# Float64 tiles five ahead on another queue, block 0's stores moved, and smaller rings in a two-MLP kernel

## The chip, the cores and the metric

The kernel runs on one core of a Trainium2 chip. The metric is the device time of one execution in microseconds (us). The engines are named as in the profile: PE is TensorE's matmul, PEld its weight load, DVE is VectorE, ACT ScalarE, POOL GpSimd, SP SyncE; a q behind the name (ACTq, SPq) is that engine's instruction queue, which also issues DMAs, in its order.

## What is computed

Packed attention in float32 and two gated MLPs over its 4608 rows. The arrays of q, k, v and p are float32; the four weight matrices are float64 (512 x 2048 and back).

```python
def sm_attn(qq, kk, vv):
    s = scale * np.matmul(qq, kk.transpose(0, 1, 3, 2))
    s = s - np.max(s, axis=-1, keepdims=True)
    a = np.exp(s)
    a = a / (np.sum(a, axis=-1, keepdims=True) + 1e-09)
    return np.matmul(a, vv)
p_packed = sm_attn(p, k, v)            # 8 batches x 8 heads, 32 packed rows
out = sm_attn(q, p_packed, p_packed)   # 576 rows, 64 columns a head
x = out.transpose(0, 2, 1, 3).reshape(4608, 512)
h = x @ w_in;  x = (h / (1 + exp(-h))) @ w_out              # first MLP
h = x @ w_in2; y = (h * clip(h + 3, 0, 6) / 6) @ w_out2     # second MLP
```

## The kernel before

**Tiling.** The 4608 tokens are nine blocks of 512. In each block the first MLP runs over NF = 16 slices of 128 hidden columns: three hidden matmuls per product (L820 to L822, into hps), ScalarE's activation (L828) and gate (gh L835, gl DVE L836), three projecting matmuls (L843 to L845, into acc). Each float32 factor is split into a high and a low part, and a product is three matmuls: high by low, low by high, high by high. Attention for the coming batches is woven between these groups by a planner (it interleaves by place and cost; the order on TensorE is the same before and after the change).

**Block 0 converts the first MLP's weights.** Feed goes through 32 keys, alternately ("in", f) and ("out", f). load_raw (L142, DMA at L145) brings a tile of float64 as pairs of int32; conv_begin (L170, L171, ACT), conv_bits (L176, L177, DVE), conv_add (L182, POOL) rebuild a float32; conv_end (L195 ACT the high part, L196 DVE or POOL the low) gives win, wr or wo. One advance works on four neighbouring keys in these states. Feed.ahead says how many keys the loads stand ahead: RAW - 1 = 3, with RAW = 4 tiles of the tag raw. spare_raw takes tiles of the same tag for two small arrays. The split weights that later blocks want are stored to DRAM (w1i and w1o) by keep (L189), one advance or more after their split; next_in (L216, wi) and next_out (L228, wo) load them back. The calls 12 to 15 of block 0 each load one wi tile ahead; next_out waits until all kept stores are issued and the last projections have begun.

**Blocks 1 to 8** load wi and wo as they go. Blocks up to 7 use w_in fused with the packed attention values (fuse_steps, L615 and L616: fused, xf, xh, xl). Beside them Prep converts the second MLP's weights in 32 units: load (L257, praw, two DMAs on ACT), conv_begin, conv_bits, sums for a scheme of seven products, a cast and a difference (hi7 tiles), and three stores w2in or w2out (L301 to L303, on ACT). One step of Prep, some ten to a unit, follows each hidden slice; what is left at the end of block 8 is done at once by prep.end.

**Second** is the second MLP, from 942 us to the end: six pairs of N = 384 tokens each, two times two blocks by seven products. Each pair has a hidden half (28 chunks of 12 matmuls: L1058 to L1060, on xc; then the bank is added on DVE: hu L1020, h L1029, hv L1023, and gated: ACT hr L1004, DVE g L1007), a few operands made ready (t1 L1077, split L1099 ACT and L1100 DVE: ro), and a project half (28 chunks: L1136 to L1138, on ro; outputs o, ou, ov). ws, a ring of WS = 7 chunks of weights, is loaded by SP (L942) one chunk for each used. x_steps makes the next pair's xc: it loads xr (L961), makes three differences (xe, L966 to L970) and splits seven operands (L974, L975), one step at each second chunk of the project half. soon(n, ...) runs a function n steps later.

**Queues.** A DMA is issued by the engine that the code names, in that engine's order. The program gives DMAs the semaphores of eight lanes in turn, over all queues, and a DMA instruction waits for the one that had its lane before. SP also issues q, k, v and p of the coming batches (L317, L327, L334, L338, L345) and the x1d and output stores.

Of the kernel before, what the change touches and what calls it, by code (L numbers as in the profile page):

```python
# [18 lines left out]
def tile_pack_attention_two_mlps(ctx: ExitStack, tc, q, k, v, p, w_in1, w_out1, w_in2, w_out2, out):  # L19
# [77 lines left out]
    def spare_raw():  # L97
        return wp.tile([P, 2 * T], I32, tag="raw", name="raw", bufs=RAW).bitcast(F32)
# [44 lines left out]
    def load_raw(key, src):  # L143
        raw = wp.tile([P, 2 * T], I32, tag="raw", name="raw", bufs=RAW)
        nc.sync.dma_start(out=raw.rearrange("p (a f) -> p a f", a=src.shape[1]), in_=src)  # L145
        raws[key] = raw
# [38 lines left out]
    def keep(behind=1):  # L185

        while len(kept) > behind:
            to, w = kept.pop(0)
            nc.scalar.dma_start(out=to, in_=w)  # L189

    def conv_end(key):
# [4 lines left out]
        (nc.vector if kind == "in" else nc.gpsimd).tensor_sub(out=w[:, 1], in0=v, in1=f32(w[:, 0]))  # L196
        made[key] = w
        if kind == "in":
            kept.append((piece_in(f), f32(w).rearrange("p n (c f) -> p n c f", c=KC)))
        elif f % 2:  # L200
            kept.append((w1o[f].rearrange("n p f -> p n f"), f32(w)))
# [8 lines left out]
    def next_in():  # L210
        if want_in:
            key = want_in.pop(0)
            t = wts.tile([P, 2, DM], F32R, tag="wi", name="wi", bufs=4)
# [7 lines left out]
    projected = [-1]  # L221

    def next_out():

        while want_out and not kept and projected[0] >= NF - 2 and (want_out[0][0] * NF + want_out[0][1]) // 2 <= (projected[0] + 1) // 2 - 1 + WO:
# [11 lines left out]
    class Prep:  # L237
# [671 lines left out]
    WS = 7  # L909

    class Second:
# [41 lines left out]
        def x_steps(self, n):  # L953
# [11 lines left out]
            e = [self.right.tile([P, 2, N], F32, tag=f"xe{i}", name=f"xe{i}") for i in range(3)]  # L965
            nc.vector.tensor_sub(out=e[0], in0=b[1, 1], in1=b[0, 1])  # L966
            nc.vector.tensor_sub(out=b[0, 1], in0=b[0, 1], in1=b[0, 0])
            yield
            nc.vector.tensor_sub(out=e[1], in0=b[1, 1], in1=b[0, 1])
            nc.vector.tensor_sub(out=e[2], in0=b[1, 0], in1=e[1])  # L970
            yield
            for k, v in (1, b[0, 0]), (6, e[1]), (5, b[0, 1]), (7, e[0]), (2, b[1, 0]), (4, e[2]), (3, b[1, 1]):
# [4 lines left out]
                yield  # L977
# [10 lines left out]
        def hidden(self, n):  # L988
# [25 lines left out]
            def after(f, k):  # L1014
# [79 lines left out]

# [337 lines left out]
```

## Time and profile before

| | us |
|---|---|
| runs | 1687.24, 1687.88, 1687.83; median 1687.83 |
| profiled execution | 1691.33 |
| its span | 1689.5 |
| PE busy in the span | 1570.1 (93%) |
| ACT busy | 804.9 (48%) |
| DVE busy | 1039.1 (62%) |
| mean granted clock | 0.977 |

The stages of the profiled execution are: start-up attention to 44 us, block 0 to 196, blocks 1 to 8 to 942, Second to 1689. A row of windows gives an engine's busy time and number of instructions in a stretch, then the granted TensorE clock, in parts of the full one (0.50 and 1.00 are its two levels; a mean in between mixes them), the mean busy share of the 16 DMA engines and what they moved. A row of waits says for which instruction's or transfer's end an engine stood, in sum, how often, and the longest. A row of the timeline ends in the idle time before the instruction and what ended it. Releasers are inferred, and a wait for several is put down to the last.

### The profile page before, as it was taken

Reading aid. Unit: us, or ns where it says so; the run is one execution under the profiler, and the core shown is the slowest. Engines: PE = TensorE matmul, PEld = TensorE weight load, DVE = VectorE, ACT = ScalarE, POOL = GpSimd, SP = SyncE. Lnnn points to the kernel's source line nnn. Section 1 sums busy time; section 2 is a strip of 40 time slices with the busy share of each in tenths; the row PEclk is TensorE's granted clock in tenths of the full one; section 3 lists DMA queues with packets and bytes.
Section 4 is the critical chain, followed back from the end, with each engine's and each line's share of the span. In section 5 each row is a group of like instructions: output and inputs, shape, how many; then the busy total and the mean of one; then the engine's idle time right before and its main releaser. Section 6 shows DMA issues by size and latency. Waiting matters only on the chain.

```text
span 1689.5 us, 23588 instructions
## 1 busy us (share of the span) xinstructions
PE 1570.1 (93%) x8396; PEld 1343.7 (80%) x8396; DVE 1039.1 (62%) x1750; ACT 804.9 (48%) x1356; POOL 216.8 (13%) x188
## 2 busy tenths in 40 slices
PE   5877899889999899999989999999999999999997
PEld 3655656667676677767868999999999999999997
DVE  5645455465556555554343479569578678677675
ACT  4756345555555455555444345345345344444443
POOL 2443311111111021112213000000000000000000
PEclk9999899899999899999999999999999999999999
DMA  7786676776769665766698687787787887887875
GB/s 192 239 254 192 217 213 184 220 209 187 194 181 242 190 195 139 208 218 204 191 311 250 195 274 243 253 294 249 252 294 249 260 286 249 274 271 251 257 252 154
DMA packets 409749, 388.01 MB, mean 230 GB/s; under 512 B 156192, under 2 KB 282144, under 8 KB 409632
## 3 DMA queue, kind: packets, MB, share of 16 engines
q1 hardware_dynamic: 271264, 252.25, 49.6%
q10 hardware_dynamic: 138368, 134.24, 25.6%
q8 instruction: 68, 1.11, 0.3%
q14 instruction: 49, 0.40, 0.1%
HBM read 324.53 MB, written 61.87 MB: 229 GB/s over the span
## 4 chain that ended last, share of the span: by engine, by line
PE 55%; DVE 16%; ACT 13%; DMA 8%; issue 3%; POOL 2%; ACTq 1%; SPq 1%; DVEq 0%; POOLq 0%
PE acc L843 5%; PE b L1137 5%; PE acc L844 5%; PE b L1138 5%; PE acc L845 5%; PE b L1136 5%; PE b L1058 4%; PE b L1060 4%; PE b L1059 4%; PE hps L820 3%; ACT hr L1004 3%; DVE g L1007 3%; PE hps L822 3%; PE hps L821 3%; DVE ro L1100 2%
## 5 line engine op out<-in xcount | busy, mean ns | idle before, releaser
L1058 PE MATMUL b<-xc,ws 128*128 128x384 f32 x672 | 229.4, 341 | 8.0 <-DVE hu L1020 8.0
L1137 PE MATMUL b<-ro,ws 128*128 128x384 f32 x672 | 227.1, 338 | 6.2 <-DVE ro L1100 6.2
L1138 PE MATMUL b<-ro,ws 128*128 128x384 f32 x672 | 225.9, 336 | 0.0
L1136 PE MATMUL b<-ro,ws 128*128 128x384 f32 x672 | 225.8, 336 | 0.0
L1060 PE MATMUL b<-xc,ws 128*128 128x384 f32 x672 | 225.1, 335 | 0.0
L1059 PE MATMUL b<-xc,ws 128*128 128x384 f32 x672 | 224.8, 335 | 0.0
L836 DVE TENSOR_TENSOR gl<-hps,gh 128x512 fp32r<-128x512 f32 x144 | 99.1, 688 | 201.0 <-ACT gh L835 201.0
L1099 ACT CAST ro<-g 128x768 fp32r<-128x768 f32 x168 | 137.3, 835 | 116.9 <-DVE g L1089 34.9
L1100 DVE TENSOR_TENSOR ro<-g,ro 128x768 fp32r<-128x768 f32 x168 | 158.0, 953 | 23.7 <-ACT ro L1099 21.0
L1058 PEld LDWEIGHTS b<-xc,ws 128*128 128x128 f32 x672 | 126.2, 188 | 13.5 <-DVE hu L1020 13.4
L1137 PEld LDWEIGHTS b<-ro,ws 128*128 128x128 f32 x672 | 126.3, 188 | 9.7 <-DVE ro L1100 9.7
L828 ACT ACTIVATE hps<-hps 128x512 f32<-128x512 f32 x144 | 84.1, 584 | 95.6 <-PE hps L822 70.2
L1059 PEld LDWEIGHTS b<-xc,ws 128*128 128x128 f32 x672 | 126.3, 188 | 0.0
L1138 PEld LDWEIGHTS b<-ro,ws 128*128 128x128 f32 x672 | 126.3, 188 | 0.0
L1136 PEld LDWEIGHTS b<-ro,ws 128*128 128x128 f32 x672 | 126.3, 188 | 0.0
L1060 PEld LDWEIGHTS b<-xc,ws 128*128 128x128 f32 x672 | 126.1, 188 | 0.0
L843 PE MATMUL acc<-gh,wr 128*128 128x512 f32 x288 | 120.5, 418 | 0.9 <-ACT gh L835 0.9
L843 PE MATMUL acc<-gh,wo 128*128 128x512 f32 x288 | 117.9, 409 | 2.9 <-ACT gh L835 2.9
L844 PE MATMUL acc<-gl,wr 128*128 128x512 f32 x288 | 115.3, 400 | 0.3 <-DVE gl L836 0.2
L844 PE MATMUL acc<-gl,wo 128*128 128x512 f32 x288 | 114.2, 397 | 0.9 <-DVE gl L836 0.8
L845 PE MATMUL acc<-gh,wr 128*128 128x512 f32 x288 | 114.6, 398 | 0.0
L845 PE MATMUL acc<-gh,wo 128*128 128x512 f32 x288 | 113.8, 395 | 0.0
(262 smaller groups left out, 3046.3 us busy)
## 6 DMA issues: line engine op xcount, KB each, us to landing
ws<-w2in SPq DMA_DIRECT2D x336, 256.0 KB, 3.9
ws<-w2out SPq DMA_DIRECT2D x336, 256.0 KB, 3.5
wi<-w1i ACTq DMA_DIRECT2D x80, 512.0 KB, 4.8
wo<-w1o ACTq DMA_DIRECT2D x64, 512.0 KB, 4.7
x1d<-x SPq DMA_DIRECT2D x18, 512.0 KB, 3.2
raw<-in_moe_w_in_dram SPq DMA_DIRECT2D x16, 512.0 KB, 5.2
raw<-in_moe_w_out_dram SPq DMA_DIRECT2D x16, 512.0 KB, 4.7
w1i<-win ACTq DMA_DIRECT2D x16, 512.0 KB, 5.3
```

Source lines behind the costliest of these rows:

```text
L836: nc.vector.tensor_sub(out=gl, in0=g, in1=f32(gh))
L843: mm(acc[e], lhsT=w[:, 0, s], rhs=gh, start=first, stop=False)
L844: mm(acc[e], lhsT=w[:, 0, s], rhs=gl, start=False, stop=False)
L845: mm(acc[e], lhsT=w[:, 1, s], rhs=gh, start=False, stop=last)
L1058: mm(ps, lhsT=wh, rhs=xs[k][:, 0, c], start=first, stop=False, skip_group_check=True)
L1059: mm(ps, lhsT=wh, rhs=xs[k][:, 1, c], start=False, stop=False, skip_group_check=True)
L1060: mm(ps, lhsT=wl, rhs=xs[k][:, 0, c], start=False, stop=last, skip_group_check=True)
L1099: nc.scalar.copy(out=t[:, 0], in_=v)
L1100: nc.vector.tensor_sub(out=t[:, 1], in0=v, in1=f32(t[:, 0]))
L1136: mm(acc[i], lhsT=wh, rhs=ro[:, 0, f], start=first, stop=False, skip_group_check=True)
L1137: mm(acc[i], lhsT=wh, rhs=ro[:, 1, f], start=False, stop=False, skip_group_check=True)
L1138: mm(acc[i], lhsT=wl, rhs=ro[:, 0, f], start=False, stop=last, skip_group_check=True)
```

## The change

Tiles of ("out", f) keys and the two spare arrays go to a tag of their own, raw2, with three buffers, so that raw and raw2 have seven together; loads stand five keys ahead, up to two in one advance, and after the start-up ScalarE's queue issues them. Stores of kept split weights move from ScalarE's queue to SyncE's. wi has five buffers; five next_in calls stand at 20 to 24. next_out goes by the state of the call before. Prep starts five steps later, hi7 has two buffers. In Second, ws has six buffers; x_steps has one buffer xe, differences made in place, and 11 steps instead of 9; t1 runs at 2 steps instead of 3, and split is two parts, at 3 and 5 instead of 4; the steps of x_steps fall on other chunks of the project half.

```diff
     def spare_raw():
-        return wp.tile([P, 2 * T], I32, tag="raw", name="raw", bufs=RAW).bitcast(F32)
+        return win0.tile([P, 2 * T], I32, tag="raw2", name="raw2").bitcast(F32)
...
     def load_raw(key, src):
-        raw = wp.tile([P, 2 * T], I32, tag="raw", name="raw", bufs=RAW)
-        nc.sync.dma_start(out=raw.rearrange("p (a f) -> p a f", a=src.shape[1]), in_=src)
+        if key[0] == "in":
+            raw = wp.tile([P, 2 * T], I32, tag="raw", name="raw", bufs=RAW)
+        else:
+            raw = win0.tile([P, 2 * T], I32, tag="raw2", name="raw2")
+        (nc.sync if early[0] else nc.scalar).dma_start(out=raw.rearrange("p (a f) -> p a f", a=src.shape[1]), in_=src)
...
             to, w = kept.pop(0)
-            nc.scalar.dma_start(out=to, in_=w)
+            nc.sync.dma_start(out=to, in_=w)
...
-            t = wts.tile([P, 2, DM], F32R, tag="wi", name="wi", bufs=4)
+            t = wts.tile([P, 2, DM], F32R, tag="wi", name="wi", bufs=5)
...
-    projected = [-1]
+    projected = [-1, -1]
...
-        while want_out and not kept and projected[0] >= NF - 2 and (want_out[0][0] * NF + want_out[0][1]) // 2 <= (projected[0] + 1) // 2 - 1 + WO:
+        now, projected[1] = projected[1], -1 if kept else projected[0]
+        while want_out and now >= NF - 2 and (want_out[0][0] * NF + want_out[0][1]) // 2 <= (now + 1) // 2 - 1 + WO:
...
             self.load(0)
-            yield
+            for _ in range(6):
+                yield
...
-                hi = self.pool.tile([P, S7, P], F32, tag="hi7", name="hi7")
+                hi = self.pool.tile([P, S7, P], F32, tag="hi7", name="hi7", bufs=2)
...
-    WS = 7
+    WS = 6
...
                     if f % 2:
-                        soon(3, lambda: self.t1(f // 2))
-                        soon(4, lambda: self.split(f // 2))
+                        soon(2, lambda: self.t1(f // 2))
+                        soon(3, lambda: self.split_hi(f // 2))
+                        soon(5, lambda: self.split_lo(f // 2))
...
-                if self.prep and s % 2 == 0 and s >= 4:
+                if self.prep and s and s // FD % 2 == 0:
                     next(self.prep, None)
...
-            if self.loaded < i + self.ahead:
-                self.load()
+            for _ in range(2):
+                if self.loaded < i + self.ahead:
+                    self.load()
...
-    feed.ahead = RAW - 1
+    feed.ahead = RAW + 1
...
-                    if 12 <= calls[0] < 16:
+                    if 20 <= calls[0] < 25:
                         next_in()
```

split_hi and split_lo are the two halves of split, ACT's cast and DVE's difference. In x_steps the three differences and seven splits are:

```diff
-            e = [self.right.tile([P, 2, N], F32, tag=f"xe{i}", name=f"xe{i}") for i in range(3)]
-            nc.vector.tensor_sub(out=e[0], in0=b[1, 1], in1=b[0, 1])
-            nc.vector.tensor_sub(out=b[0, 1], in0=b[0, 1], in1=b[0, 0])
-            yield
-            nc.vector.tensor_sub(out=e[1], in0=b[1, 1], in1=b[0, 1])
-            nc.vector.tensor_sub(out=e[2], in0=b[1, 0], in1=e[1])
-            yield
-            for k, v in (1, b[0, 0]), (6, e[1]), (5, b[0, 1]), (7, e[0]), (2, b[1, 0]), (4, e[2]), (3, b[1, 1]):
...
+            nc.vector.tensor_sub(out=e, in0=b[1, 1], in1=b[0, 1])
+            yield
+            nc.vector.tensor_sub(out=b[0, 1], in0=b[0, 1], in1=b[0, 0])
+            yield
+            split(1, b[0, 0])
+            yield
+            nc.vector.tensor_sub(out=b[0, 0], in0=b[1, 1], in1=b[0, 1])
+            yield
+            split(6, b[0, 0])
...
```

**ACT in block 0**, in the middle of the conversions, before (cr is the tile under conversion, hps and gh the activation and gate of a hidden slice, wr and win split weights, ppT a copy for attention):

```order
L828 ACTIVATE hps<-hps 128x512
L835 CAST gh<-hps 128x512
L189 DMA w1o_115<-wo 128x2x512
L195 CAST wr_1015<-cr 128x512
L216 DMA wi<-w1i_109 128x1024
L170 ACTIVATE cr<-raw 128x512
L171 ACTIVATE cr<-raw 128x512
L104 COPY ppT<-abank 128x256
```

and with the change, where line numbers lie three to seven further on:

```order
L835 ACTIVATE hps<-hps 128x512
L842 CAST gh<-hps 128x512
L148 DMA raw_1016<-in_moe_w_out_dram 128x1024
L198 CAST wr_1019<-cr 128x512
L173 ACTIVATE cr<-raw 128x512
L174 ACTIVATE cr<-raw 128x512
L104 COPY ppT<-abank 128x256
L148 DMA raw<-in_moe_w_in_dram 128x4x256
L198 CAST win<-cr 128x512
```

The store of w1o and the load of wi are gone, and loads of float64 tiles stand before the casts of split weights. **SP in the same stretch**, before, with buffer numbers (vt, nat and qt hold the coming batches' v, k and q):

```order
L317 DMA vt_983<-in_v_dram 64x4x64
L327 DMA nat_985<-in_v_dram 128x2x256
L327 DMA nat_987<-in_v_dram 128x2x256
L317 DMA qt_989<-in_q_dram 64x4x64
L338 DMA nat_991<-in_q_dram 128x4x64 x2
L338 DMA nat_994<-in_q_dram 128x4x64 x2
L145 DMA raw_1012<-in_moe_w_in_dram 128x4x256
L145 DMA raw_1044<-in_moe_w_out_dram 128x1024
L145 DMA raw_1076<-in_moe_w_in_dram 128x4x256
L145 DMA raw_1121<-in_moe_w_out_dram 128x1024
L334 DMA nat_1141<-in_k_dram 32x16x32 x4
```

and with the change:

```order
L324 DMA vt_987<-in_v_dram 64x4x64
L334 DMA nat_989<-in_v_dram 128x2x256
L334 DMA nat_991<-in_v_dram 128x2x256
L324 DMA qt_993<-in_q_dram 64x4x64
L345 DMA nat_995<-in_q_dram 128x4x64 x2
L345 DMA nat_998<-in_q_dram 128x4x64 x2
L192 DMA w1o5_115<-wo_920 128x2x512
L192 DMA w1i1_110<-win_949 256x4x128
L192 DMA w1i2_111<-win_1048 256x4x128
```

Stores of split weights (w1o and w1i) stand among the loads of q, k and v, where the loads of float64 tiles (raw) stood. **DVE in the hidden half of a pair of Second**, before (g is a gated half of an operand, ro a split operand, hu, hv and h sums of the hidden products):

```order
L1007 SCALAR_TENSOR_TENSOR g_9576<-hr,hu 128x384
L1023 TENSOR_TENSOR hv<-h_9727,b 128x384
L1024 TENSOR_TENSOR hv<-hv,b 128x384
L1007 SCALAR_TENSOR_TENSOR g_9582<-hr,hv 128x384
L1077 TENSOR_TENSOR g_9576<-g_9576,g_9575 128x768
L1100 TENSOR_TENSOR ro<-g_9575,ro 128x768
L1007 SCALAR_TENSOR_TENSOR g_9579<-hr,b 128x384
L1020 TENSOR_TENSOR hu<-h_9810,b 128x384
L1029 TENSOR_TENSOR h_9727<-h_9727,b 128x384
```

and with the change (L1103 is t1, L1032 the gate, L1128 the low half of split, L1045 hu):

```order
L1032 SCALAR_TENSOR_TENSOR g_9569<-hr,hu 128x384
L1048 TENSOR_TENSOR hv<-h_9720,b 128x384
L1049 TENSOR_TENSOR hv<-hv,b 128x384
L1103 TENSOR_TENSOR g_9569<-g_9569,g_9568 128x768
L1032 SCALAR_TENSOR_TENSOR g_9575<-hr,hv 128x384
L1032 SCALAR_TENSOR_TENSOR g_9572<-hr,b 128x384
L1045 TENSOR_TENSOR hu<-h_9804,b 128x384
L1128 TENSOR_TENSOR ro<-g_9568,ro 128x768
L1054 TENSOR_TENSOR h_9720<-h_9720,b 128x384
```

t1 stands one gate earlier, and the low half of ro behind the next subtraction into hu instead of before the gate.

## Rows read from the trace of the kernel before

**Rows 1.** Windows by stage; columns: us, busy by engine (count), granted clock, DMA share, GB/s

```profile
44.00:196.00 152.00, 121.67 (x573) 89.00 (x573) 89.34 (x128) 91.75 (x166) 66.70 (x49) 0.92 0.73 222
...
210.00:942.00 732.00, 688.05 (x3421) 517.05 (x3420) 382.06 (x763) 368.33 (x634) 126.83 (x118) 0.98 0.72 205
942.00:1690.00 748.00, 724.62 (x4181) 714.27 (x4179) 541.41 (x800) 323.31 (x517) 14.18 (x6) 1.00 0.79 256
```

**Rows 2.** Waits of PE, 44 to 210 us: waited for, total us, times, longest

```profile
PE abank L487 <- ACT ppT L104: 4.7, 1, 4.7
PE abank L365 <- DVE gl L836: 4.6, 1, 4.6
...
PE abank L496 <- DVE xf L616: 3.3, 1, 3.3
...
PE abank L609 <- ACT ppT L104: 2.6, 1, 2.6
...
PE hps L820 <- ACT d L101: 2.4, 1, 2.4
```

**Rows 3.** Waits of ACT before L170, 44 to 200 us

```profile
ACT cr L170 <- DMA raw<-in_moe_w_out_dram: 7.6, 2, 5.2
ACT cr L170 <- DMA wi<-w1i: 7.5, 1, 7.5
...
ACT cr L170 <- DMA raw<-in_moe_w_in_dram: 6.5, 1, 6.5
```

**Rows 4.** Windows of three stretches behind waits of PE

```profile
106.70:113.40 6.70, 5.41 (x14) 2.87 (x14) 4.35 (x7) 6.34 (x12) 1.95 (x2) 0.50 0.93 310
...
175.00:181.60 6.60, 6.24 (x18) 4.88 (x19) 4.96 (x7) 4.40 (x9) 4.36 (x3) 0.50 0.81 263
205.70:212.30 6.60, 6.38 (x16) 4.37 (x16) 0.45 (x2) 2.11 (x4) 0.61 (x1) 0.50 0.75 265
```

**Rows 5.** Timeline of ACT, blocks 0 to 1: start, us, instruction, [idle before <-releaser]

```profile
204.46 0.58 ACT L835 CAST gh<-hps 128x512 fp32r<-128x512 f32 x1 [4.85 <-DMA w1o<-wo]
...
210.19 0.67 ACT L170 ACTIVATE pr<-praw 128x512 f32<-128x512 f32 x1 [5.14 <-DMA praw<-in_moe_w_in_dram]
```

**Rows 6.** Waits of PE in the two-MLP part

```profile
PE b L1058 <- DVE hu L1020: 8.0, 12, 1.0
PE b L1137 <- DVE ro L1100: 6.2, 11, 0.8
```

**Rows 7.** Timeline of DVE at one wait of the hidden half

```profile
980.37 0.56 DVE L1007 SCALAR_TENSOR_TENSOR g<-hr,hv 128x384 f32<-128x384 f32 x1 [0.74 <-ACT hr L1004]
980.85 0.95 DVE L1077 TENSOR_TENSOR g<-g,g 128x768 f32<-128x768 f32 x1
981.95 0.96 DVE L1100 TENSOR_TENSOR ro<-g,ro 128x768 fp32r<-128x768 f32 x1
...
983.28 0.55 DVE L1020 TENSOR_TENSOR hu<-h,b 128x384 f32<-128x384 f32 x1
```

**Rows 8.** Timeline of PE and its weight load in the project half

```profile
1026.61 0.19 PEld L1137 LDWEIGHTS b<-ro,ws 128*128 128x128 f32 x1 [0.63 <-DVE ro L1100]
1026.61 0.44 PE L1137 MATMUL b<-ro,ws 128*128 128x384 f32 x1 [0.32 <-DVE ro L1100]
```

**Rows 9.** Timelines of ACT and PE at two windows of Prep

```profile
553.32 0.66 ACT L170 ACTIVATE pr<-praw 128x512 f32<-128x512 f32 x1 [2.51 <-issue]
...
557.82 0.80 PE L820 MATMUL hps<-a2h,fused 128*128 128x512 f32 x1 [6.08 <-DVE gl L836]
...
595.39 0.59 ACT L101 COPY T<-abank 128x512 f32<-128x512 f32 x1 [0.38 <-PE abank L431]
...
597.46 0.65 PE L451 MATMUL abank<-nat,T 128*32 128x64 f32 x32
```

**Rows 10.** DMA issues, 1340 to 1360 us: count, size, median us to landing

```profile
ws<-w2in SPq DMA_DIRECT2D x14, 256.0 KB, 5.3
```

**Rows 11.** A wait of SP's queue, 44 to 200 us

```profile
SPq L317 <- PE abank L454: 18.8, 2, 9.7
```

More of the change, by code (lines that the diff above doesn't have):

```diff
@@ L195, in conv_end @@
         nc.scalar.copy(out=w[:, 0], in_=v)
-        (nc.vector if kind == "in" else nc.gpsimd).tensor_sub(out=w[:, 1], in0=v, in1=f32(w[:, 0]))
         made[key] = w
         if kind == "in":
+            nc.vector.tensor_sub(out=w[:, 1], in0=v, in1=f32(w[:, 0]))
             kept.append((piece_in(f), f32(w).rearrange("p n (c f) -> p n c f", c=KC)))
-        elif f % 2:
-            kept.append((w1o[f].rearrange("n p f -> p n f"), f32(w)))
+        else:
+            nc.gpsimd.tensor_sub(out=w[:, 1], in0=v, in1=f32(w[:, 0]))
+            if f % 2:
+                kept.append((w1o[f].rearrange("n p f -> p n f"), f32(w)))
     def piece_in(f):
@@ L964, in x_steps, with split @@
             b = {(i, k): xr[:, 2 * i:2 * i + 2, k * N:(k + 1) * N] for i in range(2) for k in range(2)}
-            e = [self.right.tile([P, 2, N], F32, tag=f"xe{i}", name=f"xe{i}") for i in range(3)]
-            nc.vector.tensor_sub(out=e[0], in0=b[1, 1], in1=b[0, 1])
-            nc.vector.tensor_sub(out=b[0, 1], in0=b[0, 1], in1=b[0, 0])
-            yield
-            nc.vector.tensor_sub(out=e[1], in0=b[1, 1], in1=b[0, 1])
-            nc.vector.tensor_sub(out=e[2], in0=b[1, 0], in1=e[1])
-            yield
-            for k, v in (1, b[0, 0]), (6, e[1]), (5, b[0, 1]), (7, e[0]), (2, b[1, 0]), (4, e[2]), (3, b[1, 1]):
+            e = self.right.tile([P, 2, N], F32, tag="xe", name="xe")
+            def split(k, v):
                 t = self.right.tile([P, 2, 2, N], F32R, tag=f"xc{k}", name=f"xc{k}")
@@ L976, in x_steps @@
                 self.x[k] = t
-                yield
+            nc.vector.tensor_sub(out=e, in0=b[1, 1], in1=b[0, 1])
[7 more added lines that the diff above has]
+            split(6, b[0, 0])
+            yield
+            split(5, b[0, 1])
+            yield
+            split(7, e)
+            yield
+            split(3, b[1, 1])
+            yield
+            nc.vector.tensor_sub(out=b[1, 1], in0=b[1, 0], in1=b[0, 0])
+            yield
+            split(2, b[1, 0])
+            yield
+            split(4, b[1, 1])
+            yield
         def begin_step(self):
@@ L1093, in sums, with split_hi, split_lo @@
                 nc.vector.tensor_sub(out=t, in0=b21, in1=t)
+        def split_hi(self, s):
+            t = self.left.tile([P, 2, 2, N], F32R, tag="ro", name="ro", bufs=4)
+            nc.scalar.copy(out=t[:, 0], in_=self.operand(s))
+            self.ro[s] = t
+        def split_lo(self, s):
+            t = self.ro[s]
+            nc.vector.tensor_sub(out=t[:, 1], in0=self.operand(s), in1=f32(t[:, 0]))
         def split(self, s):
             if s < FD * S7:
-                t = self.left.tile([P, 2, 2, N], F32R, tag="ro", name="ro", bufs=4)
-                v = self.operand(s)
-                nc.scalar.copy(out=t[:, 0], in_=v)
-                nc.vector.tensor_sub(out=t[:, 1], in0=v, in1=f32(t[:, 0]))
-                self.ro[s] = t
+                self.split_hi(s)
+                self.split_lo(s)
         def project(self, n):
```

## The prediction

> **What bounds the kernel now.** I read the stages first, then the waits of the busiest engine, then what its releasers waited for. The windows by stage [rows 1] show two kernels in one: in the two-MLP part after 942 us TensorE (PE) is busy 724.6 of 748 us, in blocks 1 to 8 (210 to 942) 688 of 732 us, and in block 0 (44 to 196) only 121.7 of 152 us, 30.3 us idle, with a granted clock of 0.92. So block 0 has the most to give, and the last part has so much TensorE work that only its own small waits count.
>
> In block 0, TensorE's waits [rows 2] name ScalarE (ACT) in three of the rows; in the L496 row DVE's xf is itself fed by ACT. What held ACT is in its own waits [rows 3]: three rows, 21.6 us, all before L170, the first conversion of a float64 tile, all for transfers. (The row that names wi<-w1i I read as a tile's load too: one landed at the same moment.) TensorE's 4.7 us (L487) is the end of the 7.5 us wait, its 2.4 us (L820) lies in the 6.5 us wait, its 2.6 us (L609) in the 5.2 us wait, its 3.3 us (L496) in the 2.4 us wait that makes up the rest of the 7.6. After a wait the engine also runs slower: in the two stretches behind the 4.7 and the 3.3 us the granted clock is 0.50 [rows 4], the lower of its two levels (1.2 of 2.4 GHz), so a stretch of 6.7 us does the work of 3.3.
>
> **Block 0: loads five ahead, on ACT's queue; stores on SP's.** The loads are issued three keys ahead by SyncE (SP), whose queue also carries q, k and v and stops for them: a v load there waited up to 9.7 us for a matmul [rows 11]. In the change they stand in ACT's order two keys earlier, ahead of the converting instructions, and the 24 stores go to SP. What can be removed on TensorE is the sum of the four waits, 4.7 + 2.4 + 2.6 + 3.3 = 13.0 us, and the half-speed stretches behind two of them, 3.35 + 3.3 = 6.7, together 19.7, and some 1.7 for a shorter half-speed stretch behind the 2.4 us wait (an estimate, half of one like those in rows 4): 21. What is added: a load on ACT can itself stand, since a DMA instruction waits for its buffer and for the semaphore it shares with a DMA issued eight earlier in the program. That this can stop ACT is seen at the end of block 0, where the cast of gh, behind two loads of wo in ACT's order, stands 4.85 us for the store of w1o [rows 5]. No row shows it for a load of a float64 tile. The bounds: nothing, or as much as the 21.6 us that go, less what lies beside TensorE work; I take 3 us, near the lower end, because the buffer that a load takes was read two keys earlier at least, and because eight DMAs earlier is two or three keys in most places, longer than most landings (it is less where SP has just issued eight small q or k loads in a row, which the change's order has twice in this stretch). So -18 us, between -5 and -30 (the upper end: some waits of ACT for POOL in the same chain go too, as its instructions come earlier).
> Moving the stores to SP costs nothing on TensorE: they wait there for the split that DVE or POOL makes, and behind them stand loads of q, k and v with the same lead as before. The price if that cover is gone is a late k or v, bounded by 9.7 us [rows 11]; it is in the range.
> The four early wi loads of block 0, moved from its calls 12 to 15 to 20 to 24 and now five, leave the crowded stretch at 107 to 113, where the DMA share is 0.93 [rows 4], and need no other price: they are wanted only in block 1.
>
> **The boundary of blocks 0 and 1.** Today ACT issues the last stores and at once the wo loads, and stands 4.85 us for the last store [rows 5]; TensorE waits 4.6 us at L365 [rows 2] and then runs 6.6 us at clock 0.50 [rows 4], 3.3 lost. Straight after, ACT waits 5.1 us for praw, the first raw tile of Prep [rows 5], which the change loads six steps ahead of its use instead of one. The change keeps the stores off ACT and holds the wo loads back by one call. Gain 4.6 + 3.3 = 7.9, taken as -8; between -3 (the wo tiles, now later, are waited for themselves) and -10.
>
> **Blocks 1 to 8.** Five more yields move all of Prep's work five steps later; the second hi7 buffer and the fifth wi buffer only loosen. The phase matters where Prep's three w2in stores and the two conversions of the next unit fall between the softmax exponentials and the next hps on ACT. Once before, they did: ACT issued for 2.5 us, converted from 553.32 on, and TensorE stood 6.1 us before L820 [rows 9]. In the order of the change the same group stands ahead of the COPY of T in four windows, one of them behind 592. There T is ready at 595.98 and wanted at 597.46 [rows 9], 1.5 us later, and the group (2.5 us of issue and two conversions of 0.66) takes ACT 3 to 4 us; I estimate new stalls of about 5 us in all, and 3 us less at 557.8, where the group is gone. With half-speed stretches the balance is 0, between -8 and +10. The five steps more that are left to the end of block 8 are half a unit, about 3 us of work on ACT, beside TensorE work; in the range.
>
> **The two-MLP part.** In each pair's hidden half TensorE waits before L1058 on DVE: 8.0 us in 12 waits, two in each of the six pairs [rows 6]. The DVE rows before one [rows 7] show why. DVE works in order: the gate at 980.37 stood 0.74 us for ACT, then came t1 (0.95 us), then ro's low half, which could start only at 981.95 when ACT's cast was nearly done, and only then the subtraction that frees the bank, ending at 983.83. The change puts t1 into the wait for ACT, and the low half two steps behind the high one. That takes about a microsecond off each place, so the waits should go: the weight load behind such a wait stands longer than its matmul, 0.63 against 0.32 us in [rows 8], so the 8.0 us stand for 8 to 16 lost; I take 10, nearer the matmuls' own rows. In the project half there are 11 waits, 6.2 us [rows 6]. Six are at its start, where the order of DVE does not change: they stay. Five come later, where DVE's xe work stands ahead of ro; one has 0.32 us on the matmul and 0.63 on the weight load [rows 8], so five are 1.6 to 3.1 us, and I take 3; the change moves these subtractions apart. Against that one ws buffer goes: a chunk is asked for 2 us later (748 us over the 336 chunks of the stage is 2.2 us at most [rows 1]). The median landing of a chunk around the next pair's x load is 5.3 us [rows 10], against a lead of six chunks now, 13 us, and of five then, 11: nothing in most places, and up to 1 us where a chunk is queued behind x. In sum -12 to -13, taken as -13; between -9 and -17.
>
> **The sum.** -18 - 8 + 0 - 13 = -39 on the profiled execution, 1691.33 us (its span is 1689.5, 1.8 us lie around it): 1652. The median of the runs is 1687.83, 3.5 lower, so I expect 1649 to 1652 and say 1650.
>
> **Rivals.**
> A, the transfers themselves are the limit of block 0: the tiles come no sooner by another queue. For it: the DMA share is 0.93 in the stretch behind the longest wait [rows 4]. Against it: 0.73 over block 0 [rows 1], less than in the last part, and the loads wait in SP's queue, not only in the engines. Then block 0 gives 0 to -5, the boundary -3, the last part -13: about 1670.
> The Trainium skill (Trainium Kernel Development and Optimization, Key Constraints) speaks for this rival: DMAs of SP, ACT and POOL share the same 16 engines, and issuing from several saves only the issue time; by it alone the sum would be that of A, 1670, by my reading of SP's waits 1650. It doesn't speak of a queue that stops at a semaphore; whether that is what the trace shows here no run has told yet.
> B, slower: ACT's in-order queue. Each of the 26 or so loads now stands before casts that TensorE waits for; if its buffer or its semaphore comes late, because an SP DMA eight before it is itself stuck behind a v load (9.7 us [rows 11]), the whole of ACT waits. It decides when ACT's new waits reach about 21.6 + 39 - 18 = 43 us in block 0, twice what goes, that is four or five such stops of 9.7 us: then +5 or more, about 1695.
> C, the Prep collisions: if each of the four windows costs what 557.8 did, 6.1 us and a half-speed stretch of 3, four make 36, less the 9 saved: +27, leaving about -12: 1676.
> D, the parts cancel and nothing changes, 1685 to 1691.
>
> **How the numbers follow.** Forecast 0.52; A 0.24; C 0.11; B 0.08; D 0.05. The forecast's own range is 1636 to 1664; with A and C the range is 1630 to 1681, leaving out B, D and the far end of the forecast. 0.2% is 3.4 us, about what can be told from no change here. Faster: 0.52 + 0.24 + 0.11 = 0.87; same 0.05; slower 0.08.
>
> **What would show it.** Right: in block 0 ACT's waits before the first conversion fall from 21.6 to under 8 us, TensorE is busy over 0.87 of the stage, and the clock is 0.95 or more; no 4.6 us wait at L365; the L1058 wait on hu is gone and that on ro halved. Wrong: a new row of ACT's waits naming q, k or v or a load's own semaphore (A or B by its size); waits for T at the four windows (C); rows of TensorE waiting for ws chunks, which I priced at under 1 us.

## The result, and the profile after

The change is faster: 1668.06 us in the median of four runs (1664.09 to 1668.84), against 1687.53 of the kernel before (1685.36 to 1687.88), a ratio on record of 0.9878 with a 95% interval of 0.9862 to 0.9895 (the quotient of these two medians is 0.9885). By the medians that is 19.5 us, where 38 were forecast; it lies in the range.

The stages of the changed kernel's profiled execution (1664.09 us, span 1662.3), as windows; these rows answer [rows 1]. The columns are us, busy time by engine with the number of instructions, granted clock, DMA share, GB/s.

```profile
44.00:176.00 132.00, 114.60 (x572) 85.44 (x573) 97.96 (x128) 91.09 (x165) 63.81 (x49) 0.96 0.85 260
176.00:923.50 747.50, 698.60 (x3460) 524.66 (x3459) 383.64 (x767) 371.43 (x638) 128.36 (x119) 0.97 0.72 205
923.50:1662.30 738.80, 720.92 (x4177) 713.51 (x4176) 540.24 (x800) 324.88 (x516) 14.18 (x6) 1.00 0.81 260
```

Block 0 ends 20 us earlier, at 176.0 instead of 196.0, with a granted clock of 0.96 where it was 0.92; TensorE is busy 114.6 of 132 us, 0.87 of the stage. Blocks 1 to 8 take as long as before, 747.6 us against 746.9. The two-MLP part starts at 923.6 instead of 942.9, and the time from its first hidden to its last project matmul falls from 734.9 to 727.1 us.

The waits of TensorE from 40 to 210 us, answering [rows 2], and those of ScalarE to 200 us, answering [rows 3] (columns: waited for, total us, times, longest):

```profile
PE abank L478 <- DVE ppf L465: 7.3, 2, 3.7
PE hps L827 <- ACT win L198: 3.9, 1, 3.9
PE abank L406 <- ACT gh L842: 3.5, 1, 3.5
```

```profile
ACT win L198 <- POOL cr L185: 15.1, 11, 2.6
ACT a2h L101 <- DVE abank L525: 10.0, 3, 3.6
...
ACT win L198 <- DMA nat<-in_k_dram: 3.0, 1, 3.0
...
ACT win L198 <- DVE ppn L464: 2.6, 1, 2.6
...
ACT gh L842 <- DMA praw<-in_moe_w_in_dram: 1.6, 1, 1.6
```

None of the waits of [rows 2] is left, and none of ScalarE's for a float64 tile. TensorE's waits for ppf have grown from 3.5 to 7.3 us, and one for win (3.9) remains. ScalarE waits for POOL's addition (15.1 us, where it was 22.0), for the chain of attention, and 5.6 us before casts of win that read neither k nor ppn: there a load of a float64 tile, ahead of the cast, stands in ScalarE's own queue. At the boundary the 4.6 us of L365 are gone, and a wait of 3.5 us at the next stop (L406, which was L399) remains, since ScalarE's cast of gh stands 1.6 us for a transfer behind praw.

The waits of TensorE in the two-MLP part, answering [rows 6]:

```profile
PE b L1169 <- DVE ro L1128: 6.2, 6, 1.0
PE b L1084 <- DVE hv L1048: 2.1, 6, 0.4
PE b L1084 <- DVE hu L1045: 0.6, 2, 0.3
PE b L1084 <- DMA ws<-w2in: 0.2, 1, 0.2
```

The 8.0 us before the sum into hu are 0.6, but 2.1 us of waits for hv are new, and the waits for ro, which were to be halved, are the same 6.2 us in 6 instead of 11 places. One row of 0.2 us is all that the profile shows of the smaller ring of weights.

**How far one profile reaches.** The profiled execution before lies 3.8 us above its kernel's median and the one after 4.0 below, so the two traces are 27.2 us apart where the runs are 19.5. Two pairs of kernels below have the same program up to the two-MLP part and yet start it 5.6 us (the change and "gate_later") and 7.1 us apart (the kernel before and "second_only"). A stage of one profile is good to some 5 us, but for the two-MLP part, which repeats to 0.5 us.

### The profile page after: what moved, and what is told of

Same layout as the page of the kernel before. It is cut to its first block, busy times and chain, and to the rows that moved or that the text cites. A ratio compares the mean times of both kernels' runs of the same rounds, so it can differ in the third digit from the quotient of the medians.

```text
span 1662.3 us, 23562 instructions
## 1 busy us (share of the span) xinstructions
PE 1559.9 (94%) x8396; PEld 1339.8 (81%) x8396; DVE 1047.3 (63%) x1750; ACT 806.2 (48%) x1356; POOL 215.1 (13%) x188
## 4 chain that ended last, share of the span: by engine, by line
PE 57%; DVE 17%; ACT 14%; DMA 6%; issue 3%; ACTq 2%; POOL 1%; SPq 0%; DVEq 0%; POOLq 0%
PE b L1169 6%; PE b L1170 6%; PE b L1168 6%; PE acc L850 6%; PE acc L851 5%; PE acc L852 5%; ACT hr L1029 4%; DVE g L1032 4%; PE hps L827 3%; PE hps L829 3%; PE hps L828 3%; PE b L1086 2%; PE b L1084 2%; PE b L1085 2%; DVE fused L623 1%
## 5 line engine op out<-in xcount | busy, mean ns | idle before, releaser
L1128 DVE TENSOR_TENSOR ro<-g,ro 128x768 fp32r<-128x768 f32 x168 | 158.5, 951 | 8.9 <-ACT ro L1123 7.5
```

The source lines that it names most:

```text
L1128: nc.vector.tensor_sub(out=t[:, 1], in0=self.operand(s), in1=f32(t[:, 0]))
```

## Experiments

The table has the median, its ratio to the runs of the kernel before on the same chip with the 95% interval, and from one profile the end of block 0 (its last copy of x), the time from there to the first hidden matmul of the two-MLP part, and that part to its last project matmul.

| kernel | median us | ratio | block 0 ends | blocks 1 to 8 | two-MLP part |
|---|---|---|---|---|---|
| before | 1687.53 | 1 | 196.0 | 746.9 | 734.9 |
| the change | 1668.06 | 0.9878 (0.9862 to 0.9895) | 176.0 | 747.6 | 727.1 |
| loads_on_sp | 1668.37 | 0.9875 (0.9858 to 0.9892) | 177.9 | 750.6 | 727.1 |
| ahead_3 | 1669.54 | 0.9878 (0.9858 to 0.9899) | 179.1 | 749.4 | 727.2 |
| loads_before | 1668.83 | 0.9876 (0.9859 to 0.9894) | 176.3 | 748.2 | 727.4 |
| ring_of_4 | 1668.80 | 0.9878 (0.9845 to 0.9911) | 178.5 | 749.3 | 727.6 |
| stores_on_act | 1676.52 | 0.9923 (0.9903 to 0.9942) | 185.3 | 751.0 | 727.1 |
| wi_early | 1671.75 | 0.9903 (0.9879 to 0.9926) | 182.1 | 749.7 | 727.2 |
| prep_early | 1666.16 | 0.9862 (0.9839 to 0.9885) | 176.2 | 750.4 | 727.2 |
| stores_only | 1687.64 | 0.9981 (0.9967 to 0.9995) | 190.1 | 750.6 | 735.2 |
| second_only | 1680.59 | 0.9949 (0.9931 to 0.9967) | 190.5 | 745.3 | 727.2 |
| three_lines | 1663.38 | 0.9836 (0.9816 to 0.9857) | 185.7 | 751.1 | 715.5 |
| gate_later | 1653.82 | 0.9791 (0.9772 to 0.9810) | 176.0 | 753.2 | 712.6 |
| hi_store_earlier | 1642.99 | 0.9725 (0.9685 to 0.9764) | 177.9 | 737.9 | 712.7 |

The first theory was the prediction's: block 0 gains because loads of float64 tiles leave SyncE's queue (Q) or stand further ahead (L). Four runs undo parts of it.

**loads_on_sp.**

```diff
-        (nc.sync if early[0] else nc.scalar).dma_start(out=raw...
+        nc.sync.dma_start(out=raw...
```

> The change with one thing undone: the loads of float64 tiles stay on SyncE's queue throughout, still five keys ahead; the stores stay on SyncE too. In the change block 0 ended 20.0 us earlier (its last copy of x at 176.0 instead of 196.0 us), and ScalarE's 21.6 us of waits for these loads were gone. Theory Q (the queue: loads stood behind q, k and v in SyncE's order): block 0 loses 12 to 20 us again, the whole is 1680 to 1688, and ScalarE again waits over 12 us before the first conversion (L173). Theory L (the lead: five keys ahead is enough on any queue): block 0 ends within 4 us of 176, the whole is within 5 us of the change's 1668.

Measured 1668.37 us, the same as the change. Theory Q is out: which queue issues the loads makes no difference.

**ahead_3.**

```diff
-    feed.ahead = RAW + 1
+    feed.ahead = RAW - 1
```

> The change with the lead alone undone: loads three keys ahead as before, on ScalarE's queue, with the same buffers. Theory Q: ScalarE's queue alone brings the gain, block 0 ends within 5 us of 176 and the whole is 1666 to 1673. Theory L: a load is issued some 8 us later and lands after it is wanted, block 0 loses 10 to 20 us, the whole is 1678 to 1688, with ScalarE waiting 10 us or more for loads before L173.

Measured 1669.54 us, ratio the same as the change's. Five keys are not needed either.

**loads_before** has both edits.

> The change with both things about the loads undone at once: on SyncE's queue and three keys ahead. The seven buffers (raw and raw2), the stores on SyncE and the late wi loads stay. Undoing one alone cost 0 to 2 us. Theory R (queue and lead each suffice, and one of them is needed): block 0 ends 10 us or more later than 176, the whole is 1677 to 1688, ScalarE waits over 10 us before the first conversion. Theory W (the loads were late in the kernel before for what stood beside them, stores and wi loads, and the way they are issued does not matter): block 0 ends at 176 to 181, the whole is 1667 to 1673.

Measured 1668.83 us; block 0 ends at 176.3. So it is not that one of the two is needed; theory R falls. ScalarE waits 6.6 us for raw tiles, and yet block 0 ends only 0.3 us later.

**ring_of_4** undoes the buffers too: one ring of four raw tiles for all keys.

```diff
-        if key[0] == "in":
-            raw = wp.tile([P, 2 * T], I32, tag="raw", name="raw", bufs=RAW)
-        else:
-            raw = win0.tile([P, 2 * T], I32, tag="raw2", name="raw2")
-        (nc.sync if early[0] else nc.scalar).dma_start(out=raw...
+        raw = wp.tile([P, 2 * T], I32, tag="raw", name="raw", bufs=RAW)
+        nc.sync.dma_start(out=raw...
...
-    feed.ahead = RAW + 1
+    feed.ahead = RAW - 1
```

> The change with the loads of float64 tiles undone in all respects: one ring of four raw tiles for both kinds of keys, three keys ahead, SyncE's queue. Stores on SyncE, late wi loads and all else as in the change. With seven buffers the same loads (three ahead, SyncE) gave 1668.8 and an end of block 0 at 176.3. Theory B (the buffers are what counts: with four, SyncE waits for a conversion to give one free, 18 us in all in the run with three lines): block 0 ends at 184 to 188, ScalarE waits 15 to 20 us for raw tiles, the whole is 1675 to 1681. Rival (buffers do not matter; block 0's late end in the three-line kernel came from how next_out or the wi loads stood there): block 0 ends at 176 to 180, the whole is within 4 us of 1668.

Measured 1668.80 us; block 0 ends at 178.5. SyncE waits longer than ever for a free buffer, and ScalarE hardly notices (waits of SyncE to 196 us, then of ScalarE to 200, in this kernel):

```profile
SPq L145 <- DVE cr L177: 36.0, 14, 4.6
```

```profile
ACT cr L170 <- DMA raw<-in_moe_w_out_dram: 4.3, 3, 1.9
...
ACT cr L170 <- DMA raw<-in_moe_w_in_dram: 2.3, 1, 2.3
```

Theory B falls as well. Queue, lead of five and buffers, the parts that name the change, are together worth nothing that these runs can tell. All four kernels keep the change's two loads in one advance.

**stores_on_act** undoes the stores' move.

```diff
-            nc.sync.dma_start(out=to, in_=w)
+            nc.scalar.dma_start(out=to, in_=w)
```

> The change with the stores of split weights back on ScalarE's queue. If these stores held ScalarE (as the prediction had it for the boundary, 4.85 us of wait for the w1o store), the end of block 0 and the start of block 1 lose 3 to 8 us, the whole is 1671 to 1677. Rival: on SyncE they hold up q, k and v as much as they held ScalarE: within 3 us of the change, and SyncE's k load wait before the stall at 94.9 us (3.7 us on TensorE) shrinks.

Measured 1676.52 us: 8.5 us more than the change, and block 0 ends 9.3 later. ScalarE stands with a load and a store in its queue. The longest stop (timeline of ScalarE, then of TensorE: start, us, instruction, idle before and what ended it):

```profile
145.74 0.67 ACT L174 ACTIVATE cr<-raw 128x512 int32<-128x512 uint32 x1
148.63 0.34 ACTq L148 DMA_DIRECT2D raw<-in_moe_w_out_dram  x1
150.84 0.59 ACTq L192 DMA_DIRECT2D w1i<-win  x1
151.53 0.62 ACT L198 CAST win<-cr 128x512 fp32r<-128x512 f32 x1 [5.12 <-DMA qt<-in_q_dram]
...
156.21 0.45 PE L556 MATMUL abank<-a2t,ppf 128*128 128x64 f32 x1 [5.77 <-DVE a2t L534]
```

The row of the cast names a load of q, which the cast does not read. Ahead of it in ScalarE's queue a load of a float64 tile goes out only at 148.63 and the store of win at 150.84, 1.9 us after that load was out. The transposes of attention on VectorE stand behind the same tile's split, and TensorE waits 5.8 us for them. There most of the loss arises: matched by matmul, TensorE is 1.6 us behind the change before this wait and 9.3 us four us after it. A stop of 3.5 us at 104 us also has a store (of wo) ahead of the cast. At the end of block 0, where the prediction had the stores' harm, nothing more is lost: the wait at L406 is 3.5 us in both kernels.

**wi_early** puts the five wi loads of block 0 near their old place.

```diff
-                    if 20 <= calls[0] < 25:
+                    if 12 <= calls[0] < 17:
```

> The change with the five wi loads of block 0 at calls 12 to 16 instead of 20 to 24, near their old place. Theory W: the stall of 4.7 us at 103 (before L487) came from the wi loads in ScalarE's order, so block 0 loses 5 to 9 us, the whole is 1673 to 1678, and ScalarE stands for a wi load or a store near 100 us. Theory R: the loads of float64 tiles are early enough, nothing stands behind the wi loads, within 3 us of 1668.

Measured 1671.75 us, 3.7 more (the intervals overlap a little), block 0 6.1 later. ScalarE stands once for 6.1 us (timeline of ScalarE):

```profile
114.73 0.39 ACTq L148 DMA_DIRECT2D raw<-in_moe_w_in_dram  x1
115.16 0.62 ACT L198 CAST win<-cr 128x512 fp32r<-128x512 f32 x1 [6.07 <-DMA w1i<-win]
```

It is not a wi load that stands here, but a load of a float64 tile ahead of the cast; the transfer named, a store of win that SyncE issued, had the load's semaphore before it and landed at 114.71. With the wi loads moved, the DMAs between their old and their new place get others of the eight semaphores. That this is what cost the 3.7 us, and not the wi loads' own place, is not shown.

**stores_only** and **three_lines** go the other way, from the kernel before.

```diff
-            nc.scalar.dma_start(out=to, in_=w)
+            nc.sync.dma_start(out=to, in_=w)
```

> The kernel before with one line of the change: the stores of split weights on SyncE's queue (loads of float64 tiles three keys ahead on SyncE, four buffers, wi loads at calls 12 to 15). In the change, undoing the stores cost 8.4 us in the median and 9.3 us at the end of block 0 of the profile, undoing the wi loads' place 3.7 and 6.1, undoing the loads' queue and lead nothing. Theory W: the stores held ScalarE, so block 0 ends 9 to 14 us earlier than 196, at 182 to 187, the whole is 1674 to 1680. Rival (only with seven buffers, since with four the loads wait in SyncE's queue behind stores as well): block 0 ends at 191 or later, the whole is 1684 or more.

Measured 1687.64 us, where the kernel before had 1690.77 on that chip: 0.2% less, and block 0 ends at 190.1, as it also did in second_only with nothing changed there. Moving the stores alone gives little; ScalarE still waits 20.6 us for raw tiles, and TensorE's stop at L365 grows from 4.6 to 7.7 us.

```diff
-            nc.scalar.dma_start(out=to, in_=w)
+            nc.sync.dma_start(out=to, in_=w)
...
-                soon(1, gate)
+                soon(2, gate)
...
-                    if 12 <= calls[0] < 16:
+                    if 20 <= calls[0] < 24:
```

> The kernel before with three lines: stores of split weights on SyncE's queue, the four early wi loads at calls 20 to 23, and in the two-MLP part each gate one step later (as in the run before, which took that stage from 727.1 to 712.7 us on top of the change). Ring of four raw tiles, loads three keys ahead on SyncE, Prep, ws, x_steps and split as in the kernel before. Theory W and D (stores and wi loads make block 0's gain, VectorE's order makes the last stage's): block 0 ends at 176 to 181, the last stage takes 712 to 716 us, the whole is 1648 to 1656. Rivals: block 0 ends at 186 or later (the seven buffers are needed): 1658 to 1664; the last stage keeps its split and t1 waits, 720 us or more: 1656 to 1664.

Measured 1663.38 us, better than the change, with 715.5 us in the two-MLP part as theory D had it. But block 0 ends at 185.7, and ScalarE waits 18.8 us for raw tiles (its waits to 200 us):

```profile
ACT cr L170 <- DMA raw<-in_moe_w_in_dram: 10.0, 4, 4.9
...
ACT cr L170 <- DMA raw<-in_moe_w_out_dram: 8.8, 3, 4.1
```

It has the stores and wi loads of the change, and a ring of four like ring_of_4, which waits 6.6 us and ends at 178.5. What differs between the two in block 0's loads is one edit that the prediction passed over, "up to two loads in one advance". The order of SyncE's instructions shows it, three_lines first (w1i0 is a store):

```
L145 DMA raw_573<-in_moe_w_in_dram 128x4x256
L189 DMA w1i0_109<-win_479 256x4x128
L145 DMA raw_582<-in_moe_w_out_dram 128x1024
L145 DMA raw_623<-in_moe_w_in_dram 128x4x256
L189 DMA w1i0_109<-win_531 256x4x128
```

```
L145 DMA raw_573<-in_moe_w_in_dram 128x4x256
L145 DMA raw_575<-in_moe_w_out_dram 128x1024
L189 DMA w1i0_109<-win_479 256x4x128
L145 DMA raw_584<-in_moe_w_in_dram 128x4x256
L145 DMA raw_625<-in_moe_w_out_dram 128x1024
L189 DMA w1i0_109<-win_531 256x4x128
```

The start-up sets the lead to RAW - 2, two keys. The line that then says three cannot catch up, as each advance loads one key and uses one: the kernel before ran two keys ahead all through block 0, not three. With two loads in an advance the third key comes, once, and stays. That this key is what takes the waits from 18.8 to 6.6 us is read from the two kernels, which differ also in a fifth wi tile, in Prep's start and in next_out; the edit alone was not run.

What next_out does shows behind block 0, in three_lines (timeline of ScalarE, and a wait of TensorE to 215 us):

```profile
196.52 0.37 ACTq L228 DMA_DIRECT2D wo<-w1o  x1
196.93 0.59 ACT L835 CAST gh<-hps 128x512 fp32r<-128x512 f32 x1 [8.79 <-DMA w1o<-wo]
```

```profile
PE abank L365 <- DVE gl L836: 7.4, 1, 7.4
```

With the stores on SyncE and next_out as before, the last store of w1o lands 10.8 us after the last copy of x, where it was 8.0, and ScalarE stands 8.8 us (9.0 in stores_only) behind the load that needs it, where the kernel before stood 4.85. In stores_on_act the stores are on ScalarE and next_out is the change's, and ScalarE stands 0.5 us for w1o. So at the boundary the gain is next_out's, and moving the stores alone makes it worse.

**prep_early** undoes Prep's shift.

```diff
-            for _ in range(6):
-                yield
+            yield
```

> The change with Prep one step in instead of six, as before. In the change blocks 2 to 8 gave back 3.7 us of what block 1 had gained. Theory P (the shift of Prep costs, as the prediction feared): blocks 2 to 8 gain 4 us or more over the change, the whole is 1660 to 1665. Rival (the shift is what makes the start of block 1 free, as its first raw tile comes in time): block 1 loses 5 us by a wait for praw before L170's counterpart, the whole is 1670 to 1676.

Measured 1666.16 us, 1.9 less, with overlapping intervals: neither theory. In the whole the shift of five steps buys and costs nothing that can be told. In the profile the rival's wait is there: ScalarE stands 7.75 us for praw at 187 us, and TensorE behind it (its waits from 176 to 215 us, in this kernel):

```profile
PE abank L405 <- DVE T L391: 7.8, 1, 7.8
```

TensorE is 4.2 us behind the change there, 0.7 ahead of it by 840 us, and 3.0 behind it again at the start of the two-MLP part: what the shift gains at the boundary it loses in the blocks behind, within what one profile can tell.

**second_only** is the kernel before with the whole two-MLP part of the change.

> The kernel before with the change in the two-MLP part alone (ws ring of six, x_steps, t1 and the split). In the change this stage was 7.8 us shorter (first hidden to last project matmul, 734.9 to 727.1), where 13 was predicted. If the stage stands by itself: 1678 to 1681, the same 727 us in the stage. If the loads of its start or Prep's end made part of it: more than 2 us off.

Measured 1680.59 us, and 727.2 us in the part: it stands by itself, and is worth 7.7 us there and 8.0 in the median.

**gate_later** is the change with one line more.

```diff
-                soon(1, gate)
+                soon(2, gate)
```

> The change with one thing more: in the hidden half each gate stands one step later on VectorE, behind the sum that frees a bank instead of before it. In the change TensorE loses 0.6 us at each turn from hidden to project half, for hv, which stands behind a gate that waits 0.74 us for ScalarE, where it lost nothing before; six turns are 3.7 us. Theory D (VectorE's order is what paces the turn, so the waits removed from the hidden half come back there): the turn goes from 4.97 to 4.4 us, the whole is 1663 to 1666. Rival (the turn waits for ScalarE's or TensorE's own chain, or for a chunk of weights, the ring being one smaller): the turn stays at 4.9 or more, within 1.5 us of 1668.

Measured 1653.82 us, 14 less than the change, where 3.7 were expected. VectorE's waits for ScalarE's activation (hr) in the two-MLP part, in the change and then with the gate later:

```profile
DVE g L1032 <- ACT hr L1029: 110.5, 160, 1.0
```

```profile
DVE g L1032 <- ACT hr L1029: 39.5, 75, 0.7
```

TensorE has no wait left in the part, which takes 712.6 us. The windows of blocks 1 to 8 and of the part:

```profile
176.00:929.00 753.00, 701.62 (x3460) 526.71 (x3459) 383.44 (x767) 372.06 (x638) 128.95 (x119) 0.97 0.72 204
929.00:1653.60 724.60, 715.77 (x4178) 714.51 (x4176) 543.33 (x800) 325.06 (x516) 14.18 (x6) 1.00 0.83 265
```

Theory D holds, and went further than thought: the gate that stands for ScalarE 0.7 us each time, 160 times, was what kept VectorE behind at the turn, at the first project chunks and all along the hidden half of the first pair.

**hi_store_earlier** is gate_later with one of Prep's three stores a step earlier.

```diff
                 nc.gpsimd.tensor_sub(out=c[:, 3:8].bitcast(F32R), in0=c[:, 3:8], in1=hi[:, 2:7])
-                yield
-                yield
                 to = w2[kind][f].rearrange("s p f -> p s f")
+                yield
                 nc.scalar.dma_start(out=to[:, :, h * P:(h + 1) * P], in_=hi)
+                yield
                 nc.scalar.dma_start(out=to[:, 0:2, (2 + h) * P:(3 + h) * P], in_=c[:, 0:2])
```

> The change with each gate one step later (1653.8), and in Prep the store of the high parts one step before the two of the low parts, so that three DMAs in a row on ScalarE's queue become one and two. In a row the second takes 0.52 and the third 0.94 to 1.06 us to issue, the first 0.37; ScalarE stood 37 us for issue before Prep's conversions in blocks 1 to 8. Theory I (this issue time in front of ScalarE's casts costs TensorE time in blocks 1 to 8): the stage from block 0's end to the last part, 747 to 753 us in all runs so far, gets 3 us or more shorter, the whole is 1648 to 1651. Rival (it is beside TensorE's work, or the high-part store only waits elsewhere): within 2.5 us of 1653.8.

Measured 1642.99 us; the ratio is 0.0066 lower than gate_later's, 11 us. Blocks 1 to 8 take 737.9 us, 15 less than in gate_later's profile and 7 less than in any other (windows of this kernel):

```profile
178.00:916.00 738.00, 695.88 (x3461) 524.42 (x3460) 383.67 (x767) 372.63 (x638) 128.43 (x119) 0.98 0.73 208
916.00:1640.30 724.30, 715.53 (x4177) 714.32 (x4175) 543.46 (x800) 324.97 (x516) 14.47 (x6) 1.00 0.83 265
```

It is the fastest kernel of the study. Where the time was is seen at one such place in the change (timeline of ScalarE, then of VectorE and TensorE):

```profile
299.46 1.36 ACTq L309 DMA_DIRECT2D w2in<-c  x1
300.91 1.24 ACTq L310 DMA_DIRECT2D w2in<-c  x1
302.19 0.66 ACT L173 ACTIVATE pr<-praw 128x512 f32<-128x512 f32 x1 [2.63 <-issue]
302.76 0.65 ACT L174 ACTIVATE pr<-praw 128x512 int32<-128x512 uint32 x1
303.30 0.56 ACT L622 CAST fused<-abank 64x512 fp32r<-64x512 f32 x1
...
305.22 0.69 DVE L623 TENSOR_TENSOR raw<-abank,raw 64x512 fp32r<-64x512 f32 x1 [0.65 <-ACT raw L622]
...
306.02 0.47 PE L616 MATMUL abank<-wi,ph 128*128 128x512 f32 x1 [2.93 <-issue]
```

Two stores take 2.6 us to go out, the conversions stand behind them, and the casts and differences that empty a bank (L622, L623) behind those. TensorE waits 2.9 us at L616; the profile names no releaser, and I read it as a wait for that bank, whose last difference ends at 305.91. The waits of TensorE before L616 in blocks 1 to 8, in the change, in gate_later and in hi_store_earlier:

```profile
PE abank L616 <- issue: 9.3, 6, 2.9
```

```profile
PE abank L616 <- issue: 10.8, 6, 3.3
```

```profile
PE abank L616 <- issue: 5.6, 5, 3.3
```

And ScalarE's time for issue ahead of Prep's conversions (200 to 915 us), in gate_later and in hi_store_earlier:

```profile
ACT pr L173 <- issue: 39.8, 18, 5.7
```

```profile
ACT pr L173 <- issue: 27.4, 18, 5.6
```

ScalarE has 12.4 us of this wait less. Of the 15 us L616 accounts for 5; the rest of TensorE's gain is spread over smaller waits and over a granted clock of 0.98 instead of 0.97. Whether the space between the stores counts, or only that the first of them stands earlier, these runs don't tell.

## Why the prediction was half right

Since TensorE's order is the same before and after, each matmul can be matched, and the difference of its starts (the change's minus the kernel before's, in the two profiles) shows where time came from:

| matmul starts before at | 98 | 130 | 148 | 175 | 182 | 206 | 210 | 293 | 328 | 389 | 558 | 692 | 869 | 943 |
|---|---|---|---|---|---|---|---|---|---|---|---|---|---|---|
| shift, us | +1.1 | -6.7 | -11.3 | -17.2 | -20.0 | -24.8 | -26.7 | -21.6 | -26.1 | -20.5 | -22.6 | -17.2 | -18.5 | -19.4 |

**Block 0, -18: the size came out, the cause was wrong.** -20.0 at 182. The four waits named went, with half-speed stretches: TensorE's waits in the stage fell from 30.3 to 17.4 us. But the step "The loads are issued three keys ahead by SyncE (SP), whose queue also carries q, k and v and stops for them" failed twice: they were two ahead, and the queue did not matter. What mattered the prediction priced at nothing: the stores off ScalarE's queue (8.5 us when undone) and the place of the wi loads (3.7, at the edge of what can be told). That -18 met -20.0 is luck, of the causes and of the execution: in the profile of second_only, which has the program of the kernel before in this stage, block 0 ends at 190.5, and the gain would be 14.6.

The runs bound it better. The change takes 19.5 us off the median and the two-MLP part alone 8.0, so all that lies ahead of that part is worth some 11.5 us, where the terms made 26. Of these the stores alone bring 3.1 (stores_only), the stores and the later wi loads 8.0 (three_lines: 27.4 less the 19.4 of its two-MLP part), and the last 3 or 4 are left to the second load in an advance, next_out and the rest, which no run tells apart.

**Rival A** named the right rule and the wrong result. The Trainium skill (Trainium Kernel Development and Optimization, Key Constraints) says that issuing from several engines saves only issue time. For the loads the runs agree, 1668.37 against 1668.06 us. But the engines had room: DMA's share rose to 0.85 in a block 0 that was 20 us shorter. And "only" misleads where the issuing queue is a computing engine's: there the queue that the stores stand in was worth 8.5 us in block 0, and their place in it 11 us for Prep's.

**The boundary, -8:** -6.7 between 182 and 210, by the wait named (L365) and its half-speed stretch. Right; of the two reasons given, it was the held-back wo loads and not the stores' move (three_lines, stores_on_act).

**Blocks 1 to 8, 0:** +7.3, from -26.7 at 210 to -19.4 at 943, where the two-MLP part starts, inside the bounds given, and the term that cost most of the gain. The place was wrong: no wait for ScalarE's copy of T at the four windows, where 5 us were feared, but 9.3 us before L616 where 2.7 had been before L609, behind Prep's stores. Undoing the shift (prep_early) lost 4.2 us at the boundary, for praw, and gained 4.9 behind it up to 840 us; moving one of the three stores gained 11 on top of gate_later (hi_store_earlier). How much of it is the change's isn't settled: the profiles with the change's program in this stage, boundary included, have 747.6 to 753.2 us, those with the kernel before's 745.3 to 751.1 (before, second_only, stores_only, three_lines), so what the boundary gained is given back or lies within that spread.

**The two-MLP part, -13:** -7.8. The waits of the hidden half went as worked out: 9.8 us by the lengths of the six halves. The step that failed is "Six are at its start, where the order of DVE does not change: they stay." They grew from 0.77 to 1.03 us each, while the five later ones went. With TensorE faster, VectorE's chain was late at the turn. The timeline of VectorE and TensorE there, in the change:

```profile
983.22 0.56 DVE L1032 SCALAR_TENSOR_TENSOR g<-hr,hu 128x384 f32<-128x384 f32 x1 [0.74 <-ACT hr L1029]
983.70 0.55 DVE L1048 TENSOR_TENSOR hv<-h,b 128x384 f32<-128x384 f32 x1
...
984.30 0.44 PE L1084 MATMUL b<-xc,ws 128*128 128x384 f32 x1 [0.33 <-DVE hv L1048]
...
990.17 0.96 DVE L1103 TENSOR_TENSOR g<-g,g 128x768 f32<-128x768 f32 x1
991.04 1.82 DVE L1128 TENSOR_TENSOR ro<-g,ro 128x768 fp32r<-128x768 f32 x2
...
992.05 0.45 PE L1169 MATMUL b<-ro,ws 128*128 128x384 f32 x1 [1.03 <-DVE ro L1128]
```

The gate waits 0.74 us for ScalarE, hv starts only behind it, and TensorE stands for hv; later t1 stands before ro, and TensorE waits 1.0 us for ro. From hidden to project half the gap grew from 4.37 to 4.97 us; the six turns gave back 3.4 us of the 9.8, and the project halves, with the longer first stop, gained 1.4 instead of 3. Of the ring of six the profile shows 0.2, as priced.

**The sum:** the terms were -18, -8, 0, -13; the profiles show -20.0, -6.7, +7.3, -7.8, together -27.2. The median then lost 7.7 more, which lies in the two profiled executions and not in a stage.

**Rivals B, C and D** did not come. B's mechanism is there with 5.6 us of ScalarE's waits, near the 3 priced and far from the 43 that it needed; C's mechanism, Prep's bunch on ScalarE, is there at another place, with 7.3 us for the whole stage instead of 27.

## What to carry to other kernels

A DMA issued from a computing engine stands in that engine's order with all that it waits for, so ask what its queue does next before asking how early the data comes; here a place one step earlier for one of three such stores was worth 11 us. On an engine that works in order, put the instruction that another engine waits for ahead of one that has to wait itself: one step of delay for the gates was worth more than the whole change in that part. Check a lead that a program states by the order of its instructions, and read a stage's gain from more than one profile.

## What the runs showed of the hardware

DMA instructions in a row on one queue took longer to go out. In gate_later, Prep's three stores on ScalarE's queue took 0.38, 0.52 and 0.94 us (medians of the 16 w2in stores of each kind); with a step between the first and the others (hi_store_earlier) the second took 0.40 and the third 0.46. For the w2out stores the second stayed at 0.52 and the third fell from 1.06 to 0.79. All 96 stores took 69.8 us to go out in gate_later and 56.5 in hi_store_earlier. The Trainium skill (Perfetto Trace Analysis, DMA Instruction — HWDGE) has such an instruction's shown time hold a wait for the descriptor generator, which two sequencers share; no run here tells that wait from others.

Two programs that are the same up to 923 us (the change and gate_later) stayed within 0.4 us of each other up to 190 us and were 5.6 us apart at the end of block 8. The difference grew and shrank by steps of 1 to 4 us. In two of these the granted clock differs: it is 1.00 in the change and 0.79 in gate_later between 302 and 312 us, 0.99 and 0.83 between 850 and 870.
